# Block-causal attention with a gated MLP on one core: from the fifth slot on, GpSimd multiplies the probabilities by their inverse row sums ahead of the transpositions

## The chip, the cores and the metric

The kernel runs on one core of a Trainium2 chip. The metric is the device time of one execution in microseconds (us); three executions of the kernel before took 768.85, 771.0 and 771.5, median 771.0. The engines are named as in the profile: PE (TensorE, matrix products and transpositions), DVE (VectorE), ACT (ScalarE), POOL (GpSimd), SP (the queue that issues the DMAs).

## The reference, cut to what matters

```python
# q, k, v: (8 batches, 8 heads, 576 positions, 64)
mask = block_i >= block_j                       # blocks of 64 positions
scores = where(mask, q @ k.T / sqrt(64), -1e9)
scores = scores - max(scores, axis=-1)
attn = exp(scores)
attn = attn / (sum(attn, axis=-1) + 1e-09)      # the division that the change moves
x = attn @ v                                    # heads side by side: (8, 576, 512)

h = gelu(x @ w_in)                              # 512 -> 1024, split in u and v
v_n = (v - mean(v)) / sqrt(var(v) + 1e-6) * g_ln
v_s = w_sg @ v_n + b_sg                         # 576 x 576, over positions
out = x + (u * v_s) @ w_out
```

Everything is float32.

## The kernel before, in words

**Tiling.** Two heads of one batch make a pair; there are 32 pairs, numbered n = 0 to 31, and the loop of line 822 has one slot per pair. The 576 query rows of a head are cut in five row groups i = 0 to 4 (64 rows, then four times 128). Group i attends to EXT[i] = 64, 192, 320, 448, 576 key positions. The tile prob[a][i] holds the scores of head a and group i, and after the exponential the probabilities that are not yet normalised, with queries on the partitions. In the profile the ten tiles read `prob`; in listings of the order they read `prob_i_...`, where `prob_4_113` is group 4 of head 0 and `prob_4_123` group 4 of head 1. Below "4a0" stands for group 4 of head 0.

**A slot, in PE's order.** In slot n PE first turns the probabilities of pair n, so that keys come to the partitions: pA (four 128x128 transpositions per head, all of group 4), pB (five per head, the rest of group 4 and all of group 3), pC (groups 1 and 2) and pd (group 0), lines 415 to 423 and 436 to 456. Between these stand "holes" that are filled with pieces of the feed-forward work of an earlier batch: the tiles accv (5 pieces), accu (8), accs (8) and acco (8). Then come the first scores of pair n+1 (groups 4, 1 and 0, tile s), the products of pair n with v (tile ob, and group 0 into a piece of another bank), and the second scores of pair n+1 (groups 3 and 2). `PLAN` and `FIRST` (lines 711, 712) say how many pieces go in which hole: before pB, before pC, after pd, and at the slot's end, that is between the second scores and the next pair's pA. The last number is 1 to 4, and 2 or 1 in the slots of accv and in most of slots 4 to 7.

**Softmax.** DVE takes the maxima (two instructions each: the masked copy into prob, and a read of `negm`), ACT takes the exponential in place and its accumulator writes the row sum into a column of the tile `sums`. After the second scores, `inverse` (line 425) adds 1e-9 and takes the reciprocal of all ten columns on DVE (tile r, 128x10), and ACT spreads them over 128x640 elements (tile rx). In `turn_sums` PE transposes the five 128x128 pieces of rx too (three into the bank pd, two into the bank pe), ACT copies the result to rb, and `normalise` multiplies the products by rb while it takes them out of PSUM.

**Float32 products.** Each is done as three with a high and a low part (hi*hi, lo*hi, hi*lo). POOL makes the parts: a cast (kh, qh, wi_h, ws_h, wo_h) and a subtraction (kl, ql, wi_l, ws_l, wo_l, xl, gl). The weights are split this way during the first slots; `load_share` and the table WS place the last pieces in slots 4 to 8.

**What sets the order.** PE runs everywhere in program order. On DVE, ACT and POOL the program's order holds for slots 0 to 3 only; from slot n == Q = 4 on (line 824) a scheduler chooses the order ahead of time, and each engine then runs its own list strictly from front to back. So a delayed instruction holds up all that stands behind it on its engine.

Of the kernel before, what the change touches and what calls it, by code (L numbers as in the profile page):

```python
# [9 lines left out]
F32 = mybir.dt.float32  # L10
# [4 lines left out]
ALU = mybir.AluOpType  # L15
# [5 lines left out]
def kernel(  # L21
# [13 lines left out]
    B, H, D, S = qT.shape  # L35
    P = 128
    BLK = 64
# [10 lines left out]
    QN = [BLK] + [P] * (NT - 1)  # L48
    EXT = [BLK + P * i for i in range(NT)]
    written = set("P")  # L50

    class Engine:


        def __init__(self, letter, engine):
            self.letter, self.engine = letter, engine
# [5 lines left out]
    vector = Engine("V", nc.vector)  # L62
    scalar = Engine("A", nc.scalar)
    gpsimd = Engine("G", nc.gpsimd)
# [3 lines left out]
    sp = ctx.enter_context(tc.tile_pool(name="sp", bufs=1))  # L68
# [7 lines left out]
    def page(dtype, n, name):  # L76
        tag, bufs = KINDS.get(name, KINDS["w"])
        return sp.tile([P, n], dtype, tag=tag, name=name, bufs=bufs)

    def bank(name):  # L80
        return psum.tile([P, 512], F32, tag="bank", name=name, bufs=8)
# [7 lines left out]
    def turn(out, in_):  # L89
        return tensor.transpose(out, in_, ident)  # L90

    def copy(e, dst, src):
        f = {"v": vector.tensor_copy, "a": scalar.copy, "g": gpsimd.tensor_copy}[e]
        return f(dst, src)
# [63 lines left out]
    for s in (0, 1):  # L158
        t = cp.tile([P, NT, 2 * D], F32, name=f"v_f{s}")
        gpsimd.memset(t[TAIL:, NT - 1, :], 0.0)  # L160
        v_bufs.append(t)
    prob = []
    for s in (0, 1):
        row = []
        for i in range(NT):
            t = cp.tile([P, P * (i + 1)], F32, name=f"prob{s}_{i}")
# [125 lines left out]
    def weight_half():  # L292

        while weights:
            said = next(weights[0][1], None)
            if said is not None:
                return said
            weights.popleft()
# [16 lines left out]
    class Scores:  # L315


        def __init__(self, n):
            self.qh, self.ql, self.kh, self.kl = qk.pop(n)
            self.sm = sp.tile([P, NT, 2], F32, tag="sums", name="sums", bufs=3)  # L320
            gpsimd.memset(self.sm[:, 0, :], 1.0)
            self.negm = [
                sp.tile([P, NT], F32, tag=f"negm{a}", name="negm", bufs=2) for a in (0, 1)
            ]
            self.where = {}
# [38 lines left out]
        def exponent(self, a, i):  # L364
            r, e = slice(0, QN[i]), EXT[i]
            behind["A"] = scalar.activation(
                prob[a][i][r, :e],
                prob[a][i][r, :e],
                AF.Exp,
                bias=self.negm[a][r, i : i + 1],  # L370
                scale=-1.0,
                accum_out=self.sm[r, i, a : a + 1],
            )

        def step(self, *parts):
# [18 lines left out]
        def second(self):  # L394
            self.step((3, 0, EXT[3]))
            self.step((2, 0, EXT[2]))

    TE = {(0, "A"): "a", (1, "A"): "v", (0, "B"): "a", (1, "B"): "v", (0, "C"): "v", (1, "C"): "a"}
    PLACES = {
# [5 lines left out]
    class Values:  # L405
# [9 lines left out]
        def turn(self, a, which):  # L415
# [4 lines left out]
            pt = sp.tile([P, 512], F32, tag="pt", name="pt" + which, bufs=6)  # L420
            copy(TE[a, which], pt, t)
            for i, j, c in PLACES[which]:
                self.pt[a, i, j] = pt[:, c + BLK : c + P] if i == j else pt[:, c : c + P]

        def inverse(self):

            r = sp.tile([P, NT * 2], F32, tag="ri", name="r", bufs=2)
            vector.tensor_scalar_add(r, self.sm.rearrange("p i a -> p (i a)"), 1e-9)
            vector.reciprocal(r, r)
            self.rx = sp.tile([P, NT, 2 * D], F32, tag="rx", name="rx", bufs=1)  # L430
            scalar.copy(
                self.rx.rearrange("p i (a d) -> p (i a) d", a=2),
                r.unsqueeze(2).broadcast_to([P, NT * 2, D]),
            )

        def turn_sums(self):

            def spread(i):
                return self.rx[:, i, :]

            t, t2 = bank("pd"), bank("pe")
            for a in (0, 1):
                turn(t[:, a * BLK : a * BLK + P], prob[a][0])
            for i in (0, 1, 2):
                c = 2 * BLK + (i and BLK + P * (i - 1))
                turn(t[:, c : c + P], spread(i))
            for i in (3, 4):
                turn(t2[:, P * (i - 3) : P * (i - 2)], spread(i))
            w = 2 * BLK + EXT[2]
            d = sp.tile([P, 2 * BLK + S], F32, tag="rb", name="rb", bufs=1)  # L450
            copy("a", d[:, :w], t[:, :w])
            copy("a", d[:, w:], t2[:, : 2 * P])
            for a in (0, 1):
                self.pt[a, 0, 0] = d[:, a * BLK : (a + 1) * BLK]
            self.rb = d[:, 2 * BLK :]
            self.o0 = t2[:, 2 * P : 2 * P + BLK]
# [20 lines left out]
        def normalise(self):  # L477

            x = self.x = page(F32, S, "x")
            vector.tensor_tensor(x[:, BLK:], self.ob, self.rb[:, BLK:], op=ALU.mult)  # L480
            vector.tensor_tensor(x[:, :BLK], self.o0, self.rb[:, :BLK], op=ALU.mult)
            spill[self.b, self.p] = dp.tile([P, S], F32, tag="spill", name="spill", bufs=12)
            nc.sync.dma_start(spill[self.b, self.p], x)

# [14 lines left out]
    def run_side(k):  # L499

        while k > 0 and side and side[0][0] != "G":
            k -= 1
            side.popleft()[1]()
# [198 lines left out]
    def load_share(n, k):  # L702

        if n in WS:
            with ExitStack() as order:
                for ins in behind.values():
                    order.enter_context(tc.issue_after(ins.ins))
                for _ in range(WS[n][k]):
                    weight_step()

    PLAN = ["1112", "2114", "2114", "2114"]
    FIRST = ["1112", "1111", "1111", "2114"]
    Q = H // 2

    def split_pending():

# [4 lines left out]
    def opening_slot(n, va):  # L721
# [18 lines left out]
        weight_half()  # L740
        if n < Q - 1:
            nx.second()
# [11 lines left out]
        nv = Values(n + 1, nx)  # L754
        if n == Q - 1:
            nv.inverse()
# [3 lines left out]
    def slot(n, va):  # L760
        nx = n + 1 < N
        k = 6 if n // Q == 1 else 3
        g = [int(x) for x in (FIRST if n // Q == 1 else PLAN)[n % Q]]
        if n + 1 < N:
# [26 lines left out]
        load_share(n, 2)  # L791
        if n == Q + 1:
            run_side(2 * NT + 1)
        if n % Q == Q - 1:
            va.split()
# [81 lines left out]
```

## Time and profile before

One execution was profiled. It took 770.48 us; its span from the first to the last instruction is 768.7 us, at a mean granted TensorE clock of 0.993 of full.

| | value |
|---|---|
| median of three executions | 771.0 us |
| the profiled execution | 770.48 us |
| its span | 768.7 us |
| DVE busy | 483.5 us, 63% |
| ACT busy | 438.3 us, 57% |
| DMA, mean over the span | 86 GB/s |

Busy time is summed over the span, and a busy PE is one with a matrix product in flight. Rows of a timeline give start, duration, engine, line, operation, the tile written and the tiles read, the shape, and how many such instructions follow one another; square brackets at the end hold the idle time before it and what ended that. Nearly all rows have line 60, a helper, so the tiles' names tell them apart.

### The profile page before, as it was taken

Reading aid. Unit: us, or ns where it says so; the run is one execution under the profiler, and the core shown is the slowest. Engines: PE = TensorE matmul, PEld = TensorE weight load, DVE = VectorE, ACT = ScalarE, POOL = GpSimd, SP = SyncE. Lnnn points to the kernel's source line nnn. Section 1 sums busy time; section 2 is a strip of 40 time slices with the busy share of each in tenths; the row PEclk is TensorE's granted clock in tenths of the full one; section 3 lists DMA queues with packets and bytes.
Section 4 is the critical chain, followed back from the end, with each engine's and each line's share of the span. In section 5 each row is a group of like instructions: output and inputs, shape, how many; then the busy total and the mean of one; then the engine's idle time right before and its main releaser. Section 6 shows DMA issues by size and latency. Waiting matters only on the chain.

```text
span 768.7 us, 18262 instructions
## 1 busy us (share of the span) xinstructions
PE 751.7 (98%) x7106; PEld 711.2 (93%) x7106; DVE 483.5 (63%) x1477; ACT 438.3 (57%) x1096; POOL 299.2 (39%) x382
## 2 busy tenths in 40 slices
PE   8779998999999999999999999999999999999998
PEld 8778997989999899999999899998999989998998
DVE  6898789775945468544776348663495644942632
ACT  6666868558734767337754377544874467731600
POOL 3666695544234333243434234341234522322121
PEclk9989999999999999999999999999999999999999
DMA  8235233224232213312242112511124211120032
GB/s 261 82 103 178 64 107 92 77 90 133 85 119 62 63 64 109 94 47 63 64 140 78 33 61 76 172 48 48 49 91 141 63 42 53 53 88 17 1 124 93
DMA packets 46922, 65.84 MB, mean 86 GB/s; under 512 B 4082, under 2 KB 22514, under 8 KB 46836
## 3 DMA queue, kind: packets, MB, share of 16 engines
q1 hardware_dynamic: 46836, 64.67, 27.0%
q8 instruction: 56, 0.92, 0.5%
q14 instruction: 30, 0.25, 0.1%
HBM read 45.78 MB, written 18.87 MB: 84 GB/s over the span
## 4 chain that ended last, share of the span: by engine, by line
PE 92%; DVE 6%; ACT 1%; issue 1%; DMA 0%; POOL 0%; SPq 0%; DVEq 0%; ACTq 0%; POOLq 0%
PE accs L60 15%; PE accv L60 14%; PE acco L60 13%; PE accu L60 12%; PE s L60 10%; PE ob L60 10%; PE pB L60 5%; PE pC L60 5%; PE pA L60 3%; PE pd L60 2%; DVE w L60 2%; DVE prob L60 2%; PE pe L60 1%; ACT prob L60 1%; DVE vv L566 1%
## 5 line engine op out<-in xcount | busy, mean ns | idle before, releaser
L60 ACT ACTIVATE prob<-prob,negm 128x576 f32<-128x576 f32 (+3 forms) x320 | 176.4, 553 | 72.2 <-DVE negm L60 69.4
L60 DVE CUSTOM_DVE_ANT_0 prob<-s,mask 128x288 f32<-128x288 f32 (+3 forms) x320 | 121.5, 424 | 47.7 <-PE s L60 47.0
L60 POOL TENSOR_TENSOR xh<-x,xh 128x64 fp32r<-128x64 f32 x32 | 10.4, 325 | 205.5 <-DVE xh L60 145.4
L60 POOL TENSOR_TENSOR gl<-u,gh 128x288 fp32r<-128x288 f32 x64 | 51.8, 813 | 95.7 <-DVE gh L60 95.5
L60 PE MATMUL accu<-xh,wi_h 128*128 128x288 f32 x256 | 78.4, 306 | 0.0
L60 PE MATMUL accs<-ws_h,vh 128*128 128x288 f32 x256 | 77.9, 304 | 0.0
L60 PE MATMUL acco<-gh,wo_h 128*128 128x288 f32 x256 | 77.6, 303 | 0.0
L60 PE MATMUL accs<-ws_h,vl 128*128 128x288 f32 x256 | 75.6, 295 | 1.3 <-DVE vl L60 1.3
L60 PE MATMUL acco<-gl,wo_h 128*128 128x288 f32 x256 | 75.5, 295 | 0.0
L60 PE MATMUL accu<-xl,wi_h 128*128 128x288 f32 x256 | 75.5, 295 | 0.0
L60 PE MATMUL accs<-ws_l,vh 128*128 128x288 f32 x256 | 75.5, 295 | 0.0
L60 PE MATMUL accu<-xh,wi_l 128*128 128x288 f32 x256 | 75.4, 295 | 0.0
L60 PE MATMUL acco<-gh,wo_l 128*128 128x288 f32 x256 | 75.3, 294 | 0.0
L60 PE MATMUL accv<-wi_h,xh 128*128 128x512 f32 x160 | 65.3, 408 | 0.0
L60 DVE TENSOR_TENSOR u<-accs,u 128x288 f32<-128x288 f32 x64 | 29.1, 455 | 54.4 <-PE accs L60 53.9
L60 PE MATMUL accv<-wi_l,xh 128*128 128x512 f32 x160 | 63.0, 393 | 0.0
L60 PE MATMUL s<-kh,qh 64*128 64x288 f32 (+4 forms) x384 | 62.6, 322 | 0.0
L60 ACT ACTIVATION_READ_ACCUMULATOR prob<-prob,negm 128x1 f32 x320 | 59.9, 187 | 0.0
L60 PE MATMUL s<-kh,ql 64*128 64x288 f32 (+4 forms) x384 | 58.4, 301 | 0.0
L60 PE MATMUL s<-kl,qh 64*128 64x288 f32 (+4 forms) x384 | 57.3, 299 | 0.0
L60 ACT COPY vv<-accv 128x512 f32<-128x512 f32 x32 | 18.6, 581 | 67.1 <-PE accv L60 67.1
L60 PE MATMUL pB<-ident,prob 128*128 128x128 f32 x320 | 43.6, 283 | 8.5 <-DVE negm L60 6.8
(113 smaller groups left out, 2108.5 us busy)
## 6 DMA issues: line engine op xcount, KB each, us to landing
q_f<-in_qT SPq DMA_DIRECT2D x32, 288.0 KB, 3.6
k_f<-in_kT SPq DMA_DIRECT2D x32, 288.0 KB, 2.8
spill<-x SPq DMA_DIRECT2D x32, 288.0 KB, 2.9
xr<-spill SPq DMA_DIRECT2D x32, 288.0 KB, 2.9
out_T<-xr SPq DMA_DIRECT2D x32, 288.0 KB, 2.1
v_f<-in_v SPq DMA_DIRECT2D x32, 256.0 KB, 3.2
w<-in_w_in SPq DMA_DIRECT2D x16, 256.0 KB, 4.8
xr<-in_w_out SPq DMA_DIRECT2D x8, 256.0 KB, 2.7
```

The source lines that it names most:

```text
L60: return lambda *a, **k: pin(method(*a, **k), self.letter)
L566: tc.keep_in_program_order(nc.vector.scalar_tensor_tensor(x, x, stats[:rows, st, 0:1], g_bc[:rows, :], op0=ALU.subtract, op1=ALU.mult))
```

## The change: what it does

For pairs n >= 4, after DVE has the inverse sums, POOL multiplies each of the ten probability tiles by its column of r, in place, before PE turns them. The inverse comes in two halves: the columns of groups 0, 1 and 4 (128x6) as soon as the first scores' exponentials are done, the columns of groups 2 and 3 (128x4) after the second. For that the columns of `sums` are reordered (`SUM`), so that each half is contiguous. No rx is spread on ACT, no rx is transposed on PE, the bank pe isn't used, only the first 128 columns of pd go to rb, and `normalise` becomes two plain copies of the same shapes. Pairs 0 to 3 keep the old way. `Q` only moves up in the file.

```diff
-            gpsimd.memset(self.sm[:, 0, :], 1.0)
+            gpsimd.memset(self.sm[:, SUM[0], :], 1.0)
...
-                accum_out=self.sm[r, i, a : a + 1],
+                accum_out=self.sm[r, SUM[i], a : a + 1],
...
+    SUM = [0, 1, 3, 4, 2]
+    Q = H // 2
...
             r = sp.tile([P, NT * 2], F32, tag="ri", name="r", bufs=2)
+            if self.n >= Q:
+                sm = self.sm.rearrange("p i a -> p (i a)")
+                for group in ((0, 1, 4), (2, 3)):
+                    lo, hi = 2 * SUM[group[0]], 2 * SUM[group[-1]] + 2
+                    vector.tensor_scalar_add(r[:, lo:hi], sm[:, lo:hi], 1e-9)
+                    vector.reciprocal(r[:, lo:hi], r[:, lo:hi])
+                    for i in reversed(group):
+                        for a in (0, 1):
+                            x = prob[a][i][: QN[i], : EXT[i]]
+                            c = 2 * SUM[i] + a
+                            gpsimd.tensor_scalar(
+                                x, x, r[: QN[i], c : c + 1], None, op0=ALU.mult
+                            )
+                return
...
             def spread(i):
-                return self.rx[:, i, :]
-
-            t, t2 = bank("pd"), bank("pe")
+                return self.rx[:, SUM[i], :]
+
+            t, t2 = bank("pd"), bank("pe") if self.n < Q else None
             for a in (0, 1):
                 turn(t[:, a * BLK : a * BLK + P], prob[a][0])
+            if self.n >= Q:
+                d = sp.tile([P, 2 * BLK + S], F32, tag="rb", name="rb", bufs=1)
+                copy("a", d[:, : 2 * BLK], t[:, : 2 * BLK])
+                for a in (0, 1):
+                    self.pt[a, 0, 0] = d[:, a * BLK : (a + 1) * BLK]
+                self.o0 = t[:, 256 : 256 + BLK]
+                return
...
             x = self.x = page(F32, S, "x")
-            vector.tensor_tensor(x[:, BLK:], self.ob, self.rb[:, BLK:], op=ALU.mult)
-            vector.tensor_tensor(x[:, :BLK], self.o0, self.rb[:, :BLK], op=ALU.mult)
+            if self.n < Q:
+                vector.tensor_tensor(x[:, BLK:], self.ob, self.rb[:, BLK:], op=ALU.mult)
+                vector.tensor_tensor(x[:, :BLK], self.o0, self.rb[:, :BLK], op=ALU.mult)
+            else:
+                copy("v", x[:, BLK:], self.ob)
+                copy("v", x[:, :BLK], self.o0)
```

The scheduler makes new lists for DVE, ACT and POOL. Four places are shown. First PE, in slot 7, from the end of pC to the next feed-forward piece (accs); before:

```order
L60 MATMUL pd<-ident,prob_0_105 128x128
L60 MATMUL pd<-ident,prob_0_115 128x128
L60 MATMUL pd<-ident,rx 128x128 x3
L60 MATMUL pe<-ident,rx 128x128 x2
L60 MATMUL accs<-ws_h,vh 128x288
```

The same place on PE in the changed kernel:

```order
L60 MATMUL pC<-ident,prob_2_119 128x128 x3
L60 MATMUL pd<-ident,prob_0_105 128x128
L60 MATMUL pd<-ident,prob_0_115 128x128
L60 MATMUL accs<-ws_h,vh 128x288
L60 MATMUL accs<-ws_h,vl 128x288
```

The five transpositions of rx are gone, and nothing else has moved on PE. Second, DVE at the end of slot 3, from the last maxima of pair 4 on, where w is a piece of the feed-forward weights that DVE converts; before:

```order
L60 ISA negm 128x1
L60 TENSOR_SCALAR w<-w 128x256
L60 COPY ptA<-pA 128x512
L60 TENSOR_SCALAR w<-w 128x256
L60 SCALAR_TENSOR_TENSOR w<-w 128x256
L60 TENSOR_SCALAR w<-w 128x256
L60 SCALAR_TENSOR_TENSOR w<-w 128x256 x2
L60 TENSOR_SCALAR r<-sums 128x10
```

The same place on DVE in the changed kernel:

```order
L60 ISA negm 128x1
L60 TENSOR_SCALAR r<-sums 128x6
L60 TENSOR_SCALAR w<-w 128x256
L60 RECIPROCAL r<-r 128x6
L60 TENSOR_SCALAR w<-w 128x256
L60 SCALAR_TENSOR_TENSOR w<-w 128x256 x2
L60 TENSOR_SCALAR w<-w 128x256
L60 TENSOR_SCALAR r<-sums 128x4
```

The first half of the inverse stands right behind the last maximum, with one conversion between its two instructions. Third, POOL around the end of slot 5, where the spatial weights (ws) and the last of the first weights (wi) are split; before:

```order
L60 TENSOR_TENSOR ws_l<-xr,ws_h 128x576
L60 TENSOR_TENSOR wi_l<-w,wi_h 128x256 x3
L60 CAST ws_h<-xr 128x576 x2
L60 TENSOR_TENSOR ws_l<-xr,ws_h 128x576 x2
L60 CAST kh<-k_f 128x576
L60 CAST qh<-q_f 128x576
```

The same stretch of POOL's list in the changed kernel, where the multiplications are those of pair 6:

```order
L60 TENSOR_TENSOR ws_l<-xr,ws_h 128x576
L60 CAST ws_h<-xr 128x576 x2
L60 TENSOR_TENSOR ws_l<-xr,ws_h 128x576
L60 TENSOR_SCALAR prob_4_113<-prob_4_113,r 128x576
L60 TENSOR_SCALAR prob_4_123<-prob_4_123,r 128x576
L60 TENSOR_SCALAR prob_1_107<-prob_1_107,r 128x192
L60 TENSOR_SCALAR prob_1_117<-prob_1_117,r 128x192
L60 TENSOR_SCALAR prob_0_105<-prob_0_105,r 64x64
L60 TENSOR_SCALAR prob_0_115<-prob_0_115,r 64x64
L60 TENSOR_TENSOR ws_l<-xr,ws_h 128x576
```

All weight work up to the last but one whole piece of ws_l stands between the last multiplication of pair 5 (2a1) and the first of pair 6. Fourth, POOL at the last pieces of the output weights (wo), the eighth of which is used by the third pair of acco pieces; before, with the next pair's kh behind it:

```order
L60 CAST wo_h<-xr 128x256
L60 TENSOR_TENSOR wo_l<-xr,wo_h 128x256
L60 CAST wo_h<-xr 128x256
L60 TENSOR_TENSOR wo_l<-xr,wo_h 128x256
L60 CAST kh<-k_f 128x576
```

The last pieces of wo in the changed kernel's list for POOL, where the multiplications are those of pair 11:

```order
L60 TENSOR_TENSOR rs<-rs,half 128x5
L60 CAST wo_h<-xr 128x256
L60 TENSOR_TENSOR wo_l<-xr,wo_h 128x256
L60 CAST wo_h<-xr 128x256
L60 TENSOR_SCALAR prob_4_113<-prob_4_113,r 128x576
L60 TENSOR_SCALAR prob_4_123<-prob_4_123,r 128x576
L60 TENSOR_SCALAR prob_1_107<-prob_1_107,r 128x192
L60 TENSOR_SCALAR prob_1_117<-prob_1_117,r 128x192
L60 TENSOR_SCALAR prob_0_105<-prob_0_105,r 64x64
L60 TENSOR_SCALAR prob_0_115<-prob_0_115,r 64x64
L60 TENSOR_TENSOR wo_l<-xr,wo_h 128x256
```

The last piece of wo_l has come behind six multiplications of pair 11, and so behind DVE's first half of that pair's inverse.

More of the change, by code (lines that the diff above doesn't have):

```diff
@@ L712 @@
     FIRST = ["1112", "1111", "1111", "2114"]
-    Q = H // 2
     def split_pending():
```

## The prediction

> **What bounds the kernel now.** I read the page's busy line first, then the chain that ended last, then the stretches, then PE's waits. Whole rows of the page:
>
> ```profile
> PE   751.7 (98%) x7106; PEld 711.2 (93%) x7106; DVE 483.5 (63%) x1477; ACT 438.3 (57%) x1096; POOL 299.2 (39%) x382
> ```
>
> The table by stretches (start and end in us, length, then busy time of PE, PEld, DVE, ACT and POOL with counts, granted clock, DMA share, GB/s):
>
> ```profile
> 24.00:30.00 6.00, 3.59 (x18) 3.28 (x19) 5.86 (x18) 3.80 (x11) 2.98 (x6) 0.79 0.17 58
> 84.00:103.00 19.00, 19.00 (x189) 17.70 (x188) 15.24 (x48) 17.46 (x43) 17.23 (x22) 1.00 0.36 105
> 103.00:126.00 23.00, 19.89 (x208) 18.94 (x206) 22.82 (x61) 15.60 (x42) 14.48 (x15) 1.00 0.36 111
> 310.00:690.00 380.00, 380.00 (x3643) 361.30 (x3643) 224.79 (x711) 218.88 (x540) 128.71 (x149) 1.00 0.24 75
> ```
>
> From 310 to 690 us PE is busy all the time, and POOL for a third. From 84 to 103 it is otherwise: POOL is busy 17.23 of 19 us, with the splitting of the weights. And from 103 to 126 PE already stands still for 3.1 us. PE's list of waits names them:
>
> ```profile
> PE pA L60 <- ACT vh L60: 1.8, 1, 1.8
> PE accs L60 <- DVE vl L60: 1.3, 1, 1.3
> ```
>
> So the kernel is bound by PE, and the two ends of the forecast are these: what PE no longer does is gained in every slot, and where POOL has no room or is far behind, PE will wait for the multiplications. The page's 98% is an average over both kinds of stretch.
>
> **What it removes.** PE's timeline in a slot of the steady part:
>
> ```profile
> 271.27 0.38 PE L60 MATMUL pd<-ident,prob 128*128 128x128 f32 x2
> 271.49 0.49 PE L60 MATMUL pd<-ident,rx 128*128 128x128 f32 x3
> 271.81 0.38 PE L60 MATMUL pe<-ident,rx 128*128 128x128 f32 x2
> 271.95 0.38 PE L60 MATMUL accu<-xh,wi_h 128*128 128x288 f32 x1
> ```
>
> From 271.49 to 271.95 PE turns rx, 0.46 us. That goes in 28 slots: 12.9 us if nothing takes its place. The spread of rx and most of the copies to rb go from ACT, and `normalise` keeps its two instructions; neither engine sets the end (63% and 57% busy), so I count nothing for them.
>
> **What it adds: the price.** Ten TENSOR_SCALARs on POOL per pair, two each of 576, 448, 320, 192 and 64 elements per partition. The nearest rows are POOL's casts (one input), its subtractions (two inputs), and the only TENSOR_SCALAR it has (in the last row the three durations are minimum, median, maximum in ns):
>
> ```profile
> L60 POOL CAST kh<-k_f 128x576 fp32r<-128x576 f32 x31 | 20.9, 674 | 78.9 <-PE s L60 78.9
> L60 POOL CAST wo_h<-xr 128x256 fp32r<-128x256 f32 x8 | 3.2, 406 | 16.6 <-DVE xr L60 16.6
> L60 POOL TENSOR_TENSOR kl<-k_f,kh 128x576 fp32r<-128x576 f32 x31 | 45.5, 1467 | 0.3
> L60 POOL TENSOR_TENSOR xh<-x,xh 128x64 fp32r<-128x64 f32 x32 | 10.4, 325 | 205.5 <-DVE xh L60 145.4
> L60 POOL TENSOR_SCALAR rs<-stats x8: 562/650/2637, 110.4 to 719.7; 128x5 f32<-128x5 f32 x8
> ```
>
> The casts give 0.84 ns per element and 0.19 us fixed; the subtractions 2.23 ns and 0.18 us. The TENSOR_SCALAR takes 0.56 us at the least for five elements, so its fixed part may be up to that. Lower bound, the casts' line: 10 x 0.19 + 3200 x 0.84 ns = 4.6 us per pair. Upper bound, the subtractions' line: 8.9 us. I take the casts' slope, since the tile is read once, and a fixed 0.37 us, midway between 0.19 and 0.56: 0.85, 0.75, 0.64, 0.53 and 0.42 us for the five sizes, 6.4 us per pair. POOL's 299.2 us over 32 slots are 9.3 us per slot of some 23; with 6.4 that is 15.7, so its throughput does not end last. The question is when each tile is ready.
>
> The Trainium skill, "GPSIMD Engine Reference", section 4.1, speaks against the change: it would have elementwise work done on VectorE, GpSimd being about half as fast with two inputs, though roughly at line rate with one. The rows 674 and 1467 for one size agree with the second half; by the first half the sum would be that of the upper bound.
>
> **The steady slots: no wait.** The tightest are those with two accv pieces before pA (last scores, pA and pB on PE; the last of the first exponentials on ACT; POOL's next work):
>
> ```profile
> 258.50 0.31 PE L60 MATMUL s<-kl,qh 64*128 64x320 f32 x2
> 263.44 1.03 PE L60 MATMUL pA<-ident,prob 128*128 128x128 f32 x8
> 267.49 1.25 PE L60 MATMUL pB<-ident,prob 128*128 128x128 f32 x10
> 258.04 0.19 ACT L60 ACTIVATION_READ_ACCUMULATOR prob<-prob,negm 64x1 f32 x1
> 259.06 0.32 POOL L60 TENSOR_TENSOR xh<-x,xh 128x64 fp32r<-128x64 f32 x1 [15.82 <-DVE xh L60]
> ```
>
> The inverse is there at 258.6; 4a1 ends 1.7 us later, 3.1 us ahead of pA. All six multiplications end at 262.2; xh, xl, kh and qh (3.1 us) and 3a0, 3a1 (1.5) make 266.8, 0.7 us ahead of pB. At the upper bound it is 268.9, and pB, which reads head 1 some 0.5 us after it starts, waits 0.9 us, in six such slots. The other slots have four pieces there. So in slots 8 to 31 I count 24 x 0.46 = **-11.0 us**.
>
> **Slots 4 to 7: the waits.** Times are those of before; each delay shifts what follows it. Slot 4, whose pA stands right behind the second scores:
>
> ```profile
> 65.38 1.09 PE L60 MATMUL pA<-ident,prob 128*128 128x128 f32 x8
> 66.23 0.48 PE L60 MATMUL accv<-wi_h,xh 128*128 128x512 f32 x1
> 67.28 0.08 DVE L60 DVE_READ_ACCUMULATOR2_ANT negm<- 128x1 f32 x1
> 67.28 0.72 DVE L60 TENSOR_SCALAR w<-w 128x256 uint32<-128x256 uint32 x1
> ```
>
> pA was done at 66.2. Now DVE's list has the inverse behind the last maximum (67.36), with one conversion in it: about 68.0. 4a0 and 4a1 end at 69.7, the second half of pA 0.45 us later: **+3.9**. Slot 5's first exponentials end by this row of ACT, and pB begins by this row of PE:
>
> ```profile
> 82.68 0.19 ACT L60 ACTIVATION_READ_ACCUMULATOR prob<-prob,negm 64x1 f32 x1
> 90.54 1.25 PE L60 MATMUL pB<-ident,prob 128*128 128x128 f32 x10
> ```
>
> The inverse at 83.4, six multiplications to 87.0, xh to qh to 90.1, 3a0 and 3a1 to 91.6, where pB's head 1 was due at 91.1: **+0.4**.
>
> Slot 6 has the heaviest wait (POOL's kl and the last of the weight work, and PE's pA and pB):
>
> ```profile
> 88.15 1.48 POOL L60 TENSOR_TENSOR kl<-k_f,kh 128x576 fp32r<-128x576 f32 x1
> 102.08 2.82 POOL L60 TENSOR_TENSOR ws_l<-xr,ws_h 128x576 fp32r<-128x576 f32 x2
> 104.20 1.03 PE L60 MATMUL pA<-ident,prob 128*128 128x128 f32 x8
> 106.68 1.25 PE L60 MATMUL pB<-ident,prob 128*128 128x128 f32 x10
> ```
>
> From kl to the end of ws_l are 16.75 us on POOL; less one ws_l, which the new list puts later, 15.3. All that now stands between pair 5's 2a1 (ended at 92.8 after 2.8 us for groups 3 and 2 from 90.0) and pair 6's 4a0. So 4a0 starts at 108.1, 4a1 ends at 109.8, pA at 110.25 in place of 104.99: +5.3. Behind them stand 1a0 to 0a1 (1.9), ws_l (1.4), kh and qh (1.3) and 3a0, 3a1 (1.5): 115.9, so pB ends at 116.4 in place of 107.7, **+8.7** by then.
>
> Slot 7 waits for what POOL held back in slot 6. The inverse deviation rs, its second step on POOL, and PE's pA and pB:
>
> ```profile
> 112.75 1.64 POOL L60 TENSOR_TENSOR rs<-rs,half 128x5 f32<-128x5 f32 x1
> 122.77 0.63 PE L60 MATMUL pA<-ident,prob 128*128 128x128 f32 x4 [1.83 <-ACT vh L60]
> 128.55 1.25 PE L60 MATMUL pB<-ident,prob 128*128 128x128 f32 x10
> ```
>
> rs was ready at 114.4. After 115.9 POOL has 2a0, 2a1, the first step of rs, a memset, kl, ws_h, ql and then this step: 7.6 us, 123.5. DVE's vone waits for it and stands ahead of pair 7's maxima; with eight maxima, vn_t and four vl the first half of the inverse is there at about 131.0, 4a1 at 132.7, pA's end at 133.2 in place of 123.2 (+10.0). POOL then has 1.9 us of multiplications, kh, qh and twice xh and xl (4.8) before 3a0 and 3a1, so pB ends at 141.3 in place of 129.6: **+11.7**, 3.0 more than in slot 6. The old waits of 1.8 and 1.3 us are inside it.
>
> Sum of slots 4 to 7: 3.9 + 0.4 + 11.7 - 4 x 0.46 = **+14.2**. The same steps give +10.3 at the lower price and +22.8 at the upper.
>
> **Slot 10: the last piece of wo_l.**
>
> ```profile
> 183.90 0.73 POOL L60 TENSOR_TENSOR wo_l<-xr,wo_h 128x256 fp32r<-128x256 f32 x1
> 209.71 0.40 PE L60 MATMUL acco<-gh,wo_h 128*128 128x288 f32 x1
> ```
>
> It had 26 us to spare. Now it stands behind six multiplications of pair 11, and DVE's list puts that pair's maxima, four vl and two conversions of the piece ahead of the inverse: about 213.3, the multiplications to 216.9, wo_l to 217.6. PE needs it 1.5 us into this acco, at 211.2: **+6.5** (5.3 to 7.6 by price).
>
> **The clock.** In the first stretch above, after PE had waited, the granted clock is 0.79 over 6 us: 1.26 us lost. The waits of slots 4, 6 and 10 exceed 3.5 us, the wait that lies in that stretch:
>
> ```profile
> 25.95 0.33 PE L60 MATMUL pB<-ident,prob 128*128 128x128 f32 x1 [3.53 <-DVE negm L60]
> ```
>
> I add 3 x 1.26 = **+3.8**, with bounds of 2.5 (two waits) and 5.0 (four). The Trainium skill, "TensorE: Matmul & The Clock Gate", Part 1, has the clock fall to half after an idle window of about 3.4 us; the row agrees, and by the page alone a wait of 1.8 us would cost nothing more.
>
> **Sum:** -11.0 + 14.2 + 6.5 + 3.8 = +13.5 on the profiled execution's 770.5: **784 us**. The median of the runs shown is 771.0, so the two frames differ by 0.5 us. Lower price: -11.0 + 10.3 + 5.3 + 2.5 = +7.1, 777.6. Upper price: -11.0 + 22.8 + 7.6 + 5.0 + 5.4 (six waits of 0.9) = +29.8, 800. The forecast's own range is 776 to 796.
>
> **The rivals.**
>
> 1. *Faster: the waits stay hidden.* One place decides, POOL's list ahead of pair 6. If the 15.3 us of weight work there take no more than 11.4, pair 6's 4a0 starts at 104.2, when pA does, and slots 6 and 7 and the conversions that lead to slot 10 stay in time. Then -12.9 + 3.9 + 0.4 and one clock loss of 1.26: 763 us; with slot 4 hidden too, 757.6. For it speaks that some rows of the stretch are drawn out by DVE working beside them, and that slot 10 rests on a long reckoning over three engines. Against it, the work is back to back in the trace. Chance 0.2.
> 2. *POOL at the upper price.* The multiplication runs like a two-input operation, or is stretched beside DVE's (the 2637 ns for five elements above is such a row). Then some 800 us. Chance 0.15. The Trainium skill, "SBUF — State Buffer", section "Who interferes with whom", has VectorE with two inputs in SBUF and GpSimd exclude each other; the 2637 ns agree.
> 3. *The losses only match the gain*: slots 6 and 7 as forecast at the lower price, slot 10 in time and the clock unharmed: -11.0 + 10.3 = -0.7, 770 us. This would also be the time if the scheduler's lists did not do what they say. Chance 0.08.
>
> The forecast (slower, 776 to 796) keeps 0.57.
>
> **Range and chances.** 762 to 800 takes in rival 1 with slot 4 waiting; it leaves out that rival with all hidden (about half of it) and what lies above 800 in rival 2, less than 2 in 10 together. A measurement of this kernel can tell about 0.3%, 2.3 us, from no change. Slower: 0.57 + 0.15 + 0.01 of rival 3 = 0.73; same 0.07; faster 0.2.
>
> **What would show it.** In the changed profile: POOL's TENSOR_SCALARs on prob, 128x576 at 0.85 us and 128x64 at 0.42; PE's list of waits with pA and pB on POOL prob in the first 150 us, some 3.9 us in slot 4, 5.3 and 3.4 in slot 6; one wait of acco on wo_l of about 6.5 us; between 310 and 690 us no waits, and a period of four slots shorter by 1.8 us. It is wrong if POOL reaches pair 6's 4a0 before PE reaches pA, if the multiplications cost over 1.2 us for 576 elements, or if waits stand in the steady part.

## The result, and the profile after

The changed kernel takes 878.69 us (median of 4 runs, 878.48 to 880.97) against 770.57 us before: a ratio of 1.1418, 95% interval 1.139 to 1.1445. The forecast was 784 us, with a range of 762 to 800. The sign was right; the size was missed by a factor of eight, and by far more than the range allowed.

The page of the changed kernel, its busy time, granted clock and chain by engine:

```profile
PE 780.9 (89%) x6966; PEld 720.5 (82%) x6966; DVE 519.3 (59%) x1533; ACT 405.2 (46%) x1040; POOL 608.3 (69%) x662
PEclk9888889899989999999999999999999999999999
POOL 39%; PE 35%; DVE 13%; issue 8%; ACT 3%; DMA 1%; POOLq 0%; SPq 0%; DVEq 0%; ACTq 0%
```

POOL's busy time has doubled, from 299.2 to 608.3 us, and POOL now has the largest share of the chain, of which PE had 92% before. PE issues 140 instructions less, as intended, and still is busy 29 us longer: it runs at a lower clock, and it starts again after many waits. Its list of waits (total in us, number, longest):

```profile
PE pB L60 <- POOL prob L60: 41.5, 37, 4.0
PE pA L60 <- POOL prob L60: 19.9, 14, 4.7
PE s L60 <- POOL ql L60: 9.2, 9, 2.2
PE accu L60 <- DVE negm L60: 2.5, 2, 2.2
PE pC L60 <- POOL prob L60: 1.8, 6, 0.4
PE acco L60 <- POOL wo_l L60: 1.7, 1, 1.7
```

None of these rows was there before. Most are waits of the transpositions for the multiplications, and they are many and short. POOL's groups by shape show why (count, busy us, mean ns):

```profile
L60 POOL TENSOR_SCALAR prob<-prob,r 128x576 f32<-128x576 f32 x56 | 97.5, 1753 | 103.3 <-PE s L60 67.4 <-DVE r L60 32.2 <-DVE x L60 2.9
L60 POOL TENSOR_SCALAR prob<-prob,r 128x448 f32<-128x448 f32 x56 | 89.7, 1608 | 0.2 <-DVE r L60 0.2
L60 POOL TENSOR_SCALAR prob<-prob,r 128x320 f32<-128x320 f32 x56 | 69.1, 1242 | 0.0
L60 POOL TENSOR_SCALAR prob<-prob,r 128x192 f32<-128x192 f32 x56 | 43.5, 790 | 0.0
L60 POOL TENSOR_SCALAR prob<-prob,r 64x64 f32<-64x64 f32 x56 | 24.6, 452 | 0.0
```

One multiplication of 576 elements takes 1.75 us, where the prediction took 0.85. The five rows make 324.4 us, 11.6 us per pair, against 6.4 in the prediction and 8.9 at its upper bound.

Four slots of the steady part, as stretches; first the kernel before, then the changed one (columns as in the prediction):

```profile
346.80:439.00 92.20, 92.20 (x886) 87.58 (x884) 54.78 (x176) 54.31 (x134) 32.05 (x38) 1.00 0.25 78
```

```profile
417.60:519.70 102.10, 94.17 (x868) 86.88 (x866) 60.55 (x186) 49.32 (x126) 76.40 (x78) 0.98 0.23 71
```

Both begin with the products of slot 16 and end with those of slot 20. PE stood idle for no time before, and for 7.9 of 102.1 us after; the other 2.0 us of the difference are in its busy time, though it has 18 instructions less. POOL, at 76.4 us, still isn't full: it is late, not saturated.

For all comparisons below, I take from PE's timeline when the products of a slot (the first ob row) begin, and how far that is behind the same slot of the kernel before. Slots 0 to 3 are the same program in all of them; there they differ by -2.1 to +0.8 us with the granted clock of the first 60 us (0.94 to 0.89). The last column is a quarter of what is added between slot 12 and slot 28, so it is per four slots.

| kernel | slot 3 | slot 7 | slot 12 | slot 28 | per four slots | time, us |
|---|---|---|---|---|---|---|
| the change | +0.8 | +36.7 | +60.5 | +101.2 | +10.2 | 878.7 |
| e1, no multiplications | -2.0 | -1.7 | +2.1 | -5.4 | -1.9 | 765.1 |
| e2, on DVE | -0.1 | +27.8 | +37.4 | +57.9 | +5.1 | 832.2 |
| e4, from pair 8 | +0.1 | +2.4 | +21.3 | +65.3 | +11.0 | 842.5 |
| e6, two tensors | -2.0 | +24.7 | +34.9 | +40.6 | +1.4 | 814.1 |
| e7, POOL in order | -2.1 | +37.2 | +65.3 | +86.8 | +5.4 | 861.5 |
| e8, two tensors from pair 12 | -2.0 | -1.9 | -2.5 | +2.9 | +1.3 | 778.6 |
| e9, two tensors, POOL in order | 0.0 | +33.7 | +55.4 | +51.7 | -0.9 | 821.8 |
| e10, before, POOL in order | 0.0 | +10.3 | +10.3 | +10.3 | 0.0 | 780.8 |
| e12, e9 from pair 12 | +0.8 | +9.4 | +8.9 | +5.4 | -0.9 | 775.4 |
| e15, e12 with late order | -1.5 | -1.5 | -2.1 | -5.9 | -0.9 | 764.5 |

So the change loses 60 us up to slot 12 and another 48 in the twenty slots from there. Both parts were to be explained. The kernels before that ran beside these had medians of 769.95 to 771.88. The runs e3, e4, e7, e9, e10 and e13 are single executions; single executions of the kernel before lie between 768.28 and 773.99.

### The profile page after: what moved, and what is told of

Same layout as the page of the kernel before. It is cut to its first block, busy times and chain, and to the rows that moved or that the text cites. A ratio compares the mean times of both kernels' runs of the same rounds, so it can differ in the third digit from the quotient of the medians.

```text
span 876.7 us, 18374 instructions
## 1 busy us (share of the span) xinstructions
PE 780.9 (89%) x6966; PEld 720.5 (82%) x6966; DVE 519.3 (59%) x1533; ACT 405.2 (46%) x1040; POOL 608.3 (69%) x662
## 3 DMA queue, kind: packets, MB, share of 16 engines
q1 hardware_dynamic: 46836, 64.67, 23.8%
## 4 chain that ended last, share of the span: by engine, by line
POOL 39%; PE 35%; DVE 13%; issue 8%; ACT 3%; DMA 1%; POOLq 0%; SPq 0%; DVEq 0%; ACTq 0%
POOL prob L60 25%; PE accs L60 6%; PE accv L60 6%; PE s L60 5%; PE accu L60 4%; PE ob L60 4%; DVE prob L60 4%; PE acco L60 4%; POOL xl L60 3%; PE pC L60 3%; PE pB L60 3%; ACT prob L60 2%; DVE gh L60 2%; POOL qh L60 2%; DVE w L60 2%
## 5 line engine op out<-in xcount | busy, mean ns | idle before, releaser
L60 POOL TENSOR_SCALAR prob<-prob,r 128x576 f32<-128x576 f32 (+1 forms) x280 | 322.5, 1169 | 103.4 <-PE s L60 67.4
L60 PE MATMUL pB<-ident,prob 128*128 128x128 f32 x320 | 55.3, 302 | 50.1 <-POOL prob L60 41.5
L60 PEld LDWEIGHTS pB<-ident,prob 128*128 128x128 f32 x320 | 38.8, 151 | 63.2 <-POOL prob L60 52.7
L60 PE MATMUL accu<-xh,wi_h 128*128 128x288 f32 x256 | 80.4, 314 | 2.5 <-DVE negm L60 2.5
L60 PE MATMUL acco<-gh,wo_h 128*128 128x288 f32 x256 | 79.5, 311 | 0.7 <-DVE xr L60 0.7
L60 PE MATMUL acco<-gh,wo_l 128*128 128x288 f32 x256 | 77.3, 302 | 1.7 <-POOL wo_l L60 1.7
L60 PE MATMUL acco<-gl,wo_h 128*128 128x288 f32 x256 | 77.5, 303 | 0.0
L60 PE MATMUL accu<-xl,wi_h 128*128 128x288 f32 x256 | 77.3, 302 | 0.0
L60 PE MATMUL s<-kh,ql 64*128 64x288 f32 (+4 forms) x384 | 60.5, 308 | 9.2 <-POOL ql L60 9.2
L60 DVE COPY ptB<-pB 128x512 f32<-128x512 f32 x32 | 22.0, 688 | 61.4 <-PE pB L60 61.4
```

Of the source, the lines that this page charges most:

```text
L60: return lambda *a, **k: pin(method(*a, **k), self.letter)
```

## The experiments

**The removal alone, e1.** The loop over the groups does nothing but the inverse; the multiplications are left out.

```diff
-                            gpsimd.tensor_scalar(
-                                x, x, r[: QN[i], c : c + 1], None, op0=ALU.mult
-                            )
+                            pass
```

> Everything of the change but the 280 multiplications, which are left out (so the output is not normalised from pair 4 on). Price theory (the removal gives what PE's timeline said, and all of the loss comes from how long POOL's multiplications take): -28 x 0.46 = -12.9 us, about 758, PE without waits after 70 us. Order theory (the scheduler's new lists and the earlier half of the inverse cost time by themselves): above 764, with waits of PE left in slots 4 to 11.

765.11 us against 769.95, a ratio of 0.9938 (0.9909 to 0.9967). Four slots of the steady part (slots 16 to 20), and two of its waits:

```profile
347.00:437.40 90.40, 90.19 (x868) 85.48 (x866) 55.01 (x184) 49.14 (x126) 34.14 (x38) 1.00 0.25 80
```

```profile
PE acco L60 <- ACT ptB L60: 2.4, 1, 2.4
PE s L60 <- POOL ql L60: 2.4, 1, 2.4
```

Both theories had a point. The period is 90.4 us in place of 92.2: the removal gives 1.8 us per four slots, the 0.46 us per slot of the prediction. But up to slot 12 the kernel loses 4.1 us (from -2.0 to +2.1), with waits that before does not have and no multiplication to blame. Two of them are the largest. In slot 6 the scores wait 2.4 us for ql, because a cast of ws_h ahead of it on POOL took 3.40 us (0.67 in the kernel before) while DVE centred v beside it:

```profile
106.76 3.40 POOL L60 CAST ws_h<-xr 128x576 fp32r<-128x576 f32 x1
106.94 3.77 DVE L591 SCALAR_TENSOR_TENSOR vv<-vv,stats,g_bc 128x512 f32<-128x512 f32 x5
```

In slot 10 acco waits 2.4 us for the copy ptB, which stands on ACT behind an activation of vh that waited 4.1 us for rs. The new lists and the inverse in two halves bring these instructions together; e1 does not part the two. PE also runs at a lower clock behind such waits (see e13). This also bounds the idea: even multiplications at no cost would win under 1% with these lists.

**The same multiplications on VectorE, e2.** `gpsimd.tensor_scalar` becomes `vector.tensor_scalar`.

> The same multiplications, in the same place of the program, on VectorE in place of GpSimd. Price theory: DVE casts 128x576 in 0.46 us in the profile of before, so ten multiplications take 2.5 to 4 us per pair instead of 11.6; DVE has room (35 of 60 us busy in the steady part), the waits of the steady slots go, some are left in slots 4 to 7: 760 to 785. Order theory (a step between the exponentials and the transpositions costs PE its cover, whichever engine does it): above 800.

832.17 against 769.95, 1.0816 (1.078 to 1.0852): the price theory missed and the order theory's "above 800" came out, though the time per pair is half (its five groups sum to 158.7 us, 5.7 us per pair, where the price theory had 2.5 to 4). In the steady part most of the loss against e1 is in one slot of four, the one with the acco pieces (27.4 us, where e1 has 22.0). ACT's timeline in slot 18, and PE's list of waits:

```profile
434.15 1.33 ACT L60 ACTIVATE vh<-vv,rs 128x512 fp32r<-128x512 f32 x2 [6.91 <-POOL rs L60]
435.39 0.56 ACT L60 COPY ptC<-pC 128x512 f32<-128x512 f32 x1
```

```profile
PE s L60 <- ACT ptC L60: 25.0, 6, 4.6
```

In ACT's list two activations of vh stand ahead of the copy of pC. They wait 6.9 us for rs, whose statistics DVE delivers late; the copy waits with them, so its bank isn't free and the next scores stand for 4.6 us. PE waits for no multiplication here. But on DVE the ten multiplications stand ahead of these statistics, which begin 14.4 us behind the products of slot 17, and 8.2 us in e1. So the time of the multiplications and the order of the lists make this loss together; e2 does not part them.

**Four forms on GpSimd, e3.** The pairs take turns:

```diff
+                            s = r[: QN[i], c : c + 1]
+                            if self.n % 4 == 0:
+                                gpsimd.tensor_scalar(x, x, s, None, op0=ALU.mult)
+                            elif self.n % 4 == 1:
+                                gpsimd.tensor_scalar(x, x, 1.0, None, op0=ALU.mult)
+                            elif self.n % 4 == 2:
+                                gpsimd.tensor_copy(x, x)
+                            else:
+                                gpsimd.tensor_tensor(
+                                    x, x, s.broadcast_to([QN[i], EXT[i]]), op=ALU.mult
+                                )
```

> On GpSimd, the same tiles in four forms, by pair: n%4=0 as in the change (a multiplication by a column), 1 a multiplication by the constant 1.0, 2 a copy in place, 3 a multiplication of two tensors with r spread by its access pattern (pairs of forms 1 and 2 are not normalised). Durations for 128x576, undisturbed. If the column operand costs: 1.65 us as now for form 0, about 0.7 us (the cast's row) for 1 and 2. If any TENSOR_SCALAR costs that: 1.65 for 0 and 1, 0.7 for 2. If working in place costs: 1.65 for all of 0, 1, 2. Form 3 at the subtraction's 1.45 us or above.

POOL's groups for 128x576 in that run, and one of the small ones:

```profile
L60 POOL TENSOR_SCALAR prob<-prob,r 128x576 f32<-128x576 f32 x14 | 24.8, 1778 | 25.7 <-PE s L60 25.0 <-DVE w L60 0.7
L60 POOL TENSOR_SCALAR prob<-prob 128x576 f32<-128x576 f32 x14 | 23.3, 1661 | 0.6
L60 POOL TENSOR_TENSOR prob<-prob,r 128x576 f32<-128x576 f32 x14 | 15.8, 1152 | 0.0
L60 POOL COPY prob<-prob 128x576 f32<-128x576 f32 x14 | 9.4, 672 | 4.0 <-ACT prob L60 4.0
...
L60 POOL TENSOR_SCALAR prob<-prob 64x64 f32<-64x64 f32 x14 | 5.4, 382 | 0.0
```

So the second expectation came out for the first three forms: a constant costs nearly what a column does (1.66 and 1.78 us), and a copy in place 0.67 us, just what the cast costs. So neither the column nor working in place makes the price, but the operation: TENSOR_SCALAR takes 2.5 ns per element ((1661 - 382) / 512) where the copy takes about 0.9. The surprise is the third row, against the expected 1.45 us or above: a product of two tensors, r spread by its access pattern, is a third cheaper than the one-input form. (Each form meets only one of a batch's four pairs here. Over all pairs the means are 1.75 us in the change and 1.21 us for two tensors in e6, so the difference stands.) (The run took 831.0 us.)

**From pair 8 on, e4.** The four conditions with Q become 2 * Q.

> The change from pair 8 on in place of pair 4. After the change slots 4 to 11 had lost 60 us against before and slots 12 to 31 another 48. Price theory (each steady slot pays): slots 4 to 7 give back their 36 us, slots 8 to 31 still pay 48 to 72 us: 820 to 843. Early-chain theory (a delay from the weight work of slots 4 to 8 that pulls the rest behind it): below 790.

842.46 us, in the price theory's range, at its upper end. Slots 4 to 7 are given back almost whole (+2.4 at slot 7 against +36.7), but the slots behind lose as before, +11.0 per four. No chain from the early slots pulls the rest; each slot pays by itself.

**Price and list apart: e6, e7, e9.** e6 takes the form of two tensors for all pairs from 4 on. e7 keeps TENSOR_SCALAR, but POOL in program order; e9 has both.

```diff
-            written.intersection_update("P")
+            written.intersection_update("PG")
```

> The change with the other form on GpSimd, a product of two tensors with r spread by its access pattern, for all pairs from 4 on: 6.9 us per pair (3.7 + 3.2 in the run of four forms) in place of 10.7, and close to the 6.4 that the prediction took. Price theory (only the size of that term was wrong): no waits in slots 12 to 31, which then win 0.46 us each, and slots 4 to 11 lose about what was predicted: 776 to 796. List theory (the new lists of DVE, ACT and POOL cost PE its cover even at this price, as they did with the multiplications on DVE): above 810, with waits left in the steady part.

> The change as it is, but POOL keeps the program's order to the end, as PE does; so a pair's ten multiplications stand right behind one another, ahead of xh, xl, kh, qh and of the weights of the next slot. Price theory: 3a0 and 3a1 end 3 us earlier, so pB's waits in the steady part (1.4 us) go, but kl and ql, which then stand behind all ten, come later and the scores wait instead: 850 to 890. List theory: under 830.

> The form of two tensors from pair 4 on, with POOL in program order. Price theory: the slots from 12 on win 0.46 us each, and slots 4 to 11, where the multiplications no longer stand behind 15 us of weight work, lose less than in the run of the same form with the scheduler's list: 765 to 785. List theory: the same, or less, since this removes what it blames.

e6: 814.06 against 771.88, 1.0554 (1.0521 to 1.0586). e7: 861.45. e9: 821.78 us. On e6 the list theory's expectation came out: it lies 18 us above the top of the price theory's range, with waits left in the steady part, though it is far from as slow there as the change. e7 lies in the price theory's range, and e9 above the range of both. The steady part of the two forms and two orders, per four slots, from the table:

| | scheduler's list | program order |
|---|---|---|
| TENSOR_SCALAR, 11.6 us per pair | +10.2 (change) | +5.4 (e7) |
| two tensors, 7.3 us per pair | +1.4 (e6) | -0.9 (e9) |
| none | -1.9 (e1) | |

Price and list both count. The form alone takes off 8.8 or 6.3 us, the order alone 4.8 or 2.3. Slots 16 to 20 of e6 and of e9:

```profile
382.90:476.80 93.90, 92.47 (x868) 87.11 (x866) 65.91 (x186) 49.44 (x126) 62.19 (x78) 0.98 0.25 77
```

```profile
401.30:492.60 91.30, 90.56 (x868) 85.48 (x866) 61.26 (x184) 49.25 (x126) 60.53 (x78) 1.00 0.25 79
```

POOL does the same work in both, and PE waits for no multiplication in either of these stretches. Both have a wait of acco for `negm` (0.6 us). e6 has also 0.8 us of waits of the scores for `negm`, and PE is busy 1.9 us longer for the same 868 instructions, at the lower clock. What differs is the order on POOL, and through it when DVE gets rs. In slot 18 of e6, rs stands behind xh (drawn out to 3.00 us beside DVE's centring of v), xl and ql; DVE's vone waits for it, and the maxima that give `negm` stand behind vone:

```profile
417.45 3.00 POOL L60 TENSOR_TENSOR xh<-x,xh 128x64 fp32r<-128x64 f32 x1
424.07 1.20 POOL L60 TENSOR_TENSOR rs<-rs,half 128x5 f32<-128x5 f32 x1
425.30 0.48 DVE L60 TENSOR_SCALAR vone<-vv,rs 64x512 fp32r<-64x512 f32 x1 [2.02 <-POOL rs L60]
429.52 0.41 PE L60 MATMUL s<-kh,qh 64*128 64x320 f32 x1 [0.56 <-DVE negm L60]
```

In e9 rs stands ahead of xh and xl:

```profile
439.20 1.54 POOL L60 TENSOR_TENSOR rs<-rs,half 128x5 f32<-128x5 f32 x1
440.72 0.33 POOL L60 TENSOR_TENSOR xh<-x,xh 128x64 fp32r<-128x64 f32 x1
```

The products of slot 18 began at 425.2 us in e6 and at 443.4 in e9, so this step of rs begins 1.1 us ahead of them in e6 and 4.2 in e9. In the slots up to 12, e9's order is worse than e6's list (+55.4 against +34.9). For that I made e10.

**Only the steady part, e8, and the order there, e12 and e14.** e8 is e6 with 3 * Q in the four conditions; e12 adds POOL's program order; e14 also keeps the bank pe for row group 0.

> The form of two tensors, and only from pair 12 on, after the weights are done. Price theory: 20 slots x 0.46 = -9.2 us, 760 to 763, with no waits on POOL. List theory: 771 or above, with waits of PE in each batch.

> Form of two tensors, from pair 12 on, with POOL in program order. In the run with this order and form from pair 4, each four slots from 12 on took 91.3 us against 92.2 before, and with the scheduler's list 94. If price and list are all that was wrong in the steady part: 20 slots, five times -0.9 and -0.5 for the last, so about 5 us under before, 765 to 767, a little faster. If POOL's program order costs the weight work of slots 4 to 11 something by itself: as slow as before or slower.

> The run beside it (two tensors, from pair 12, POOL in program order) with the bank pe still taken in each slot, for the products of row group 0 alone. There acco still waited 0.6 us in each batch for DVE's reading of a score bank, which before did not. If dropping the bank pe shifted the rotation of the eight banks so that acco takes a score's bank: that wait goes and each batch wins another 0.6 to 1 us, 761 to 764. If the wait has another cause: as the run beside it.

e8: 778.55 against 771.88, 1.009 (1.006 to 1.0121), with +1.3 per four slots, close to e6's, as the list theory had it: even late in the program, at the better price, the lists lose more than the removal wins. e12: 775.35 against 770.69, 1.0058 (1.0037 to 1.0079), as the second expectation had it; e14: 775.5, 1.0059 (1.0037 to 1.0082). Both win 0.9 per four slots from slot 12 on, and both had lost 8.6 us before slot 7, where nothing of the change is in them yet. The wait of acco for `negm` (0.6 us in each batch) stays with the bank pe kept, so the rotation of the banks does not explain it; its cause is open.

**The kernel before with that order, e10**, has the one line of the diff above and nothing else.

> The kernel before, with POOL in program order to the end: nothing of the change. If the order by itself holds up the weights: 5 to 25 us slower than before, with waits of PE in slots 4 to 10. If the 13 and 15 us waits of slots 6 and 9 with the multiplications in program order came from the multiplications alone: within 2 us of before.

780.75 us: it loses 10.3 us up to slot 7 and then nothing. Program order puts the weights' work of slots 4 to 7 in PE's way by itself. So that order helps in the steady part, with the multiplications in it, and harms the weights ahead of it.

**Both at their best, e15.** Two tensors, from pair 12 on; POOL keeps the scheduler's list up to slot 10.

```diff
         if n == Q:
             written.intersection_update("P")
+        if n == 3 * Q - 1:
+            written.add("G")
```

> Form of two tensors, from pair 12 on; POOL keeps the scheduler's list up to slot 10 and the program's order from slot 11 on. In the run with program order from slot 4 on, slots 4 to 7 had lost 8.5 us, as the kernel before with that order did, and slots 12 to 31 had won 4.5 us. If these two parts are independent: 764.5 to 767.5, faster than before by 0.4 to 0.8%. If the win of the later slots needs the early order: 769 or above.

764.51 us against 770.07: 0.9932 (0.991 to 0.9954). This beats both kernels, by a little. The win of 5.6 us agrees with the expectation, at its lower end: in the profiled executions 4.7 us are won from slot 7 to slot 31 (-1.5 to -6.2), and nothing is lost ahead of that.

**The clock, e13.** PE turns the identity 40 times into pair 4's pA bank before its first real transposition.

> The change as it is, but PE turns the identity 40 times ahead of pair 4's pA (about 4.4 us of work that nothing reads), where it waited 4.7 us. POOL's and ACT's lists stay the same, DVE's up to slot 6. Clock theory (a wait of that length also costs 6.8 us at half the clock behind it): the products of pair 4 start 2 to 3.5 us earlier against the start of pair 4's pA, and the clock in the 10 us behind it is full. If only the wait itself cost: no earlier, or later by what the turns exceed the wait.

The wait's place and what follows, as stretches: from the last scores to pA, 6.7 us from pA on, then to the products. First the change, then e13:

```profile
65.90:71.00 5.10, 0.40 (x7) 0.13 (x4) 5.10 (x21) 3.69 (x13) 3.99 (x4) 0.84 0.79 210
71.00:77.70 6.70, 5.88 (x21) 4.63 (x22) 2.27 (x6) 1.02 (x2) 6.70 (x8) 0.61 0.22 82
77.70:87.30 9.60, 9.60 (x73) 8.22 (x71) 1.86 (x5) 3.10 (x6) 9.43 (x14) 1.00 0.22 61
```

```profile
64.83:69.80 4.97, 4.83 (x46) 4.40 (x42) 4.97 (x21) 3.73 (x13) 3.85 (x4) 1.00 0.74 223
69.80:76.50 6.70, 4.94 (x26) 3.65 (x26) 2.46 (x6) 1.50 (x4) 6.70 (x8) 1.00 0.21 77
76.50:86.10 9.60, 8.98 (x65) 7.63 (x64) 1.83 (x5) 2.51 (x5) 9.43 (x13) 1.00 0.24 63
```

The clock is full where it had been 0.61, and yet nothing is won: from the last scores to the products it takes 21.4 us in the change and 21.3 in e13, and the whole kernel takes 879.21. PE only waits longer for the next tile, since POOL is busy without a gap (6.70 of 6.70) and sets the pace. The clock theory falls for this slot: where POOL sets the pace, the low clock can't be added to the waits.

Where PE sets the pace it is otherwise. Behind the wait of 2.4 us in slot 6 of e1, these are PE's products from the waiting scores to the next accu, and then the same products in the kernel before:

```profile
112.02:120.72 8.70, 8.70 (x94) 8.33 (x94) 7.33 (x26) 5.73 (x16) 3.20 (x3) 0.62 0.23 71
```

```profile
113.14:118.65 5.51, 5.51 (x97) 5.17 (x95) 5.45 (x19) 2.07 (x7) 1.25 (x2) 1.00 0.18 56
```

PE is busy without a gap in both, and in e1 it waits for nothing from there to slot 9. The same work takes 3.2 us longer at a clock of 0.62, so here the clock cost more than the wait itself.

## Why the prediction was wrong, point by point

**The removal: right.** 0.46 us per slot was predicted, and e1 shows 1.8 us per four slots.

**The price: mis-sized, and outside its bounds.** "I take the casts' slope, since the tile is read once" was the step that failed first. Whether one tile is read or two does not decide: a copy reads one and takes 0.67 us, TENSOR_SCALAR reads one and takes 1.66 to 1.78, two tensors with a spread r take 1.15. The only TENSOR_SCALAR in the profile of before had five elements and could tell nothing of a slope. I took the subtractions' line for an upper bound, 8.9 us per pair, with no row that made it one; 11.6 was measured. The Trainium skill, "GPSIMD Engine Reference", section 4.1, has one input roughly at line rate and warns of two; the copy agrees with it, TENSOR_SCALAR at 2.5 ns per element does not.

**"The steady slots: no wait": wrong, first by the price.** I had 0.7 us to spare at pB in the tightest slot. Six multiplications now take 5.75 us in place of 3.6, and 3a0 with 3a1 2.8 in place of 1.5: 3.5 us later in all, which turns the spare 0.7 into a wait of about 2.8 us; slot 17, which is of this kind, shows two waits of 1.4 and 0.6 us. And wrong also by the list: I reckoned one kind of slot through, the one with two accv pieces, took the others for safe by their four pieces, and did not read what POOL's new list puts ahead there. And I followed the multiplications to pA and pB alone, not to kl and ql, which stand behind them on POOL: the longest wait of slots 16 to 20 is that of the scores in slot 18.

```profile
464.15 0.40 PE L60 MATMUL s<-kh,ql 64*128 64x288 f32 x2 [2.19 <-POOL ql L60]
```

At 7.3 us per pair, near my price, e6 still adds 1.4 us per four slots where I had -1.8, and e9 shows that the list makes 2.3 of that.

**Contention.** I named it as a rival and priced it as the same upper bound. The change's POOL timeline has the four multiplications of groups 3 and 2 once alone and once beside DVE's centring of v, which reads two tensors; behind it that row of DVE:

```profile
430.67 4.94 POOL L60 TENSOR_SCALAR prob<-prob,r 128x448 f32<-128x448 f32 x4
451.59 7.65 POOL L60 TENSOR_SCALAR prob<-prob,r 128x448 f32<-128x448 f32 x4
```

```profile
453.94 3.36 DVE L593 SCALAR_TENSOR_TENSOR vv<-vv,stats,g_bc 128x512 f32<-128x512 f32 x5
```

POOL lost 2.7 us within DVE's 3.36, and DVE none. The Trainium skill, "SBUF — State Buffer", section "Who interferes with whom", lets VectorE with two inputs in SBUF and GpSimd's reads exclude each other; these rows agree. Against the undisturbed 5.75 + 4.94 us per pair, 28 pairs lose at most 25 of the 324.4 us this way: a small part of the price, but not of the waits. The row of 7.65 us stands on POOL ahead of the ql for which the scores of slot 18 wait 2.19 us, and without its 2.7 us that wait would not be there, if all else stays.

**Slots 4 to 7: right in place, too small in sum.** PE's timeline at the first wait of each pA and pB, and at wo_l in slot 10:

```profile
70.91 0.47 PE L60 MATMUL pA<-ident,prob 128*128 128x128 f32 x1 [4.70 <-POOL prob L60]
102.86 0.33 PE L60 MATMUL pB<-ident,prob 128*128 128x128 f32 x1 [3.98 <-POOL prob L60]
124.63 0.47 PE L60 MATMUL pA<-ident,prob 128*128 128x128 f32 x1 [4.53 <-POOL prob L60]
133.06 0.33 PE L60 MATMUL pB<-ident,prob 128*128 128x128 f32 x1 [2.52 <-POOL prob L60]
154.08 0.33 PE L60 MATMUL pA<-ident,prob 128*128 128x128 f32 x1 [2.81 <-POOL prob L60]
164.34 0.33 PE L60 MATMUL pB<-ident,prob 128*128 128x128 f32 x1 [1.33 <-POOL prob L60]
271.79 0.41 PE L60 MATMUL acco<-gh,wo_l 128*128 128x288 f32 x1 [1.69 <-POOL wo_l L60]
```

Each stands where it was forecast. With the wait for the second head behind it (0.6 to 1.3 us), slot 4 has 5.5 us (3.9 predicted), slot 5 4.6 (0.4), slot 6 5.1 and 3.1 (5.3 and 3.4), slot 7 4.1 and 2.0 (3.0 in all). Slot 5 didn't come out, since it is all price. That the waits of slot 6 did is luck. From the end of 3a1 in slot 5 to that of 4a1 POOL took 22.1 us (PE started on them at 104.24 and 126.33), where the prediction has 18.2 (91.6 to 109.8), and PE was late by nearly as much: at a clock of 0.81 it came from there to pA in 15.9 us, without a wait, where the kernel before took 13.1. By slot 7 the kernel has lost 35.9 us, against the predicted 14.2 (16.7 with two of the clock terms). Waits on POOL and on `negm` make 27 of it; the rest I put down to the lower clock, which no run parts from the waits here, 0.86 from 60 to 145 us:

```profile
60.00:145.00 85.00, 66.38 (x587) 59.02 (x585) 51.08 (x148) 39.79 (x106) 74.08 (x85) 0.86 0.27 78
```

I added 1.26 us for each wait of over 3.5 us, and both the size and the condition were wrong: where POOL sets the pace the low clock costs nothing more (e13), and where PE does, a wait of 2.4 us was followed by a loss of 3.2 (e1). How the early loss divides between the two is open. Nor is all of it the multiplications': e1, without any, loses 4.1 us up to slot 12, and e6, near my price, loses 36.9.

**Slot 10: wrong.** wo_l was waited for 1.7 us and not 6.5: PE was by then so late, from waits at pB in slots 8 to 10, that POOL nearly caught up. The slots from 7 to 12 lose 23.8 us all the same: those waits at pB make 10.0 us of it, other waits 7.0, of the scores and of acco for the most part, and the rest I put down to the lower clock.

**The range.** It was built of bounds, but of bounds for one price and for the places that I had looked at. With the price of 11.6 the steps of the prediction, continued in a straight line from 784 at 6.4 and 800 at 8.9, would still have given 817. Most of the other 60 us are in the slots that I took for safe by one example: from slot 12 on the kernel loses 48 us, where the prediction had a win of 9. The rival "POOL at the upper price" was the nearest, and had a chance of 0.15.

## What to carry to other kernels

An operation that the profile doesn't show has no upper bound by rows of other operations: the form decides (here 0.67, 1.15 and 1.75 us for the same tile), and a form is cheap to change. Work that is put between two stages of a kernel bound by another engine is judged by its latency in every kind of slot: walk through each kind along the new list, including what now stands ahead of it and what now stands behind it. And a scheduler's list is a price of its own, which can be moved: the better form, begun after the weights and kept in program order there, turned a loss of 14% into a gain of 0.7% (e15).

## What the runs showed of the hardware

In this kernel a float32 multiplication by a column or a constant takes GpSimd 2.5 ns per element of a partition, a copy in place 0.9 ((672 - 231) / 512, with 231 ns for 64x64), and a product of two tensors, one of them spread from a column, 1.7 ((1152 - 289) / 512, with 289 ns as the mean for 64x64 in the same run). I had not expected the two-input form to be the faster one. Beside five instructions of DVE that read two tensors, a cast on GpSimd took 3.40 us in place of 0.67 (e1), and four multiplications 7.65 in place of 4.94. A wait of PE of 2.4 us was followed by a stretch at a granted clock of 0.62 that cost 3.2 us (e1); in slot 4 of the change, where POOL sets the pace, a wait of 4.7 us was followed by a clock of 0.61 that cost nothing more, for with the clock full the next waits were longer by as much (e13).
